# One hand-ordered stream of slots for a two-layer attention and GLU kernel: scores of four heads into one PSUM buffer, values of 16 heads per visit, dense work in units between

## The chip, the cores and the metric

The kernel runs on one core of a Trainium2 chip. The metric is the device time of one execution in microseconds, lower is better. Engines are named as in the profile: PE is TensorE (PEld its weight loads), DVE is VectorE, ACT is ScalarE, POOL is GpSimd, SP is SyncE, which here only issues DMAs.

## The reference: two layers of windowed attention and a gated unit

```python
def _A_ref(x, wqkv, wo):              # S = 2048, D = 512, H = 32 heads of Dh = 16, W = 256
    qkv = (x @ wqkv).reshape(B, S, 3, H, Dh)...
    scores = einsum("bhqd,bhkd->bhqk", q, k) * Dh ** -0.5
    mask = (idx[:, None] - idx[None, :] >= 0) & (idx[:, None] - idx[None, :] < W)
    p = softmax(where(mask, scores, -1e9))
    return einsum("bhqk,bhkd->bhqd", p, v)... @ wo
def _B_ref(x, w_gate, w_up, w_down):  # F = 1792
    return (sigmoid(x @ w_gate) * (x @ w_up)) @ w_down
x = A_x
for _ in range(2):
    x = x + _A_ref(layernorm(x), A_wqkv, A_wo)
    x = x + _B_ref(layernorm(x), B_w_gate, B_w_up, B_w_down)
```

The two layers use the same weights. All tensors are bf16.

## The kernel before

The 2048 tokens are 16 tiles of 128 (index `t`), or four groups of 512 (`tg`). The residual `xsb` stays in SBUF. Work comes in three kinds.

*Dense work* is a list of pieces per emitter. `ProjEmitter` normalises a group (`layernorm_tiles`: statistics, a Newton root of fifteen small DVE steps, then transposes on PE through `ln_tp`), and multiplies it by q, k and v weights into `qT`, `kT` and `Vaug` (values with a column of ones per head, so that the softmax's sums come out of the same matmul). `GluEmitter` does the gate (`gps`, tanh on ACT into `gth`), the up product (`ups`), their product `hT` on DVE, and the down product (`dps`), added to `xsb`. Each unit is 4 matmuls of 512 columns, or 14 for a down tile. Weights of q, k, gate and up are loaded chunk by chunk from DRAM; half of `w_up` is written to a DRAM scratch `wuh` at the start, for sigmoid(g) u = (tanh(g/2) + 1) u/2.

*Attention* goes by key tile `t`: a key tile is met by the queries of tiles t to t+2, 384 columns. `front(t, half)` masks `kTp` out of `kT` (one copy for even and one for odd heads of each 32 rows, so that a head of 16 rows can be one of four row quarters of PE), multiplies four heads into two PSUM tiles `Sps` of two heads each (L353), takes their exp with two ACT instructions (L361) into a ring `PTring` of seven tile slots per head, and multiplies the two diagonal blocks (of queries t and t+2) by a 0/1 mask with one DVE instruction (L365). Then it makes the values of 16 heads for query tile t: head after head in the code (L378), each head a column quarter of PE, up to three key tiles accumulated.

*Normalisation and output*: `norm_half` transposes the values (`tps`), divides by the sums (`Rt`, `On`), transposes back (`tps2`, `OnT`); `oproj_fill` multiplies by `wot` (`OPps`), adds to `xsb`, and then emits dense pieces by a budget of 48 (56 for the last layer's unit).

The order of the instructions on each engine is set by the framework's scheduler, from this program order and the pools' buffers. PSUM: four banks for `Sps`, two for `oq` (values and all of normalisation), two for dense work (`glu`). The first pair of stages runs, then its remaining GLU pieces alone, and the second pair is laid over the last GLU pieces of the first.

Of the kernel before, what the change touches and what calls it, by code (L numbers as in the profile page):

```python
# [11 lines left out]
I32 = mybir.dt.int32  # L12
P = 128
VS = 18
RING_SLOTS = 7
_RING_PS = [(0, 1), (3, 1), (0, 3)]

# [10 lines left out]
class Dims:  # L28
    def __init__(self, S, D, H, Dh, F):
        self.S, self.D, self.H, self.Dh, self.F = S, D, H, Dh, F  # L30
        self.NT = S // P
        self.KT = D // P
        self.FC = F // P
        self.NCQ = D // P
        self.NCK = 2 * self.NCQ
        self.NCO = 2 * self.NCQ
        self.TGW = min(512, S)
        self.NTG = S // self.TGW
        self.NBG = self.TGW // P
        assert S % self.TGW == 0 and self.TGW % P == 0  # L40
        assert Dh == 16 and D == H * Dh and self.NCO == 8 and self.NCQ == 4
        self.VW = H * VS + 32


def make_consts(nc, cpool):
    ident = cpool.tile([P, P], BF16, name="ident")
    nc.gpsimd.memset(ident[:], 0.0)
    nc.gpsimd.affine_select(out=ident[:], in_=ident[:], compare_op=ALU.not_equal, fill=1.0,
                            base=0, pattern=[[-1, P]], channel_multiplier=1)
    maskq = cpool.tile([P, 4, 2, P], BF16, name="maskq")  # L50
    nc.gpsimd.memset(maskq[:], 1.0)
    for u in range(4):
        nc.gpsimd.affine_select(out=maskq[:, u, 0, :], in_=maskq[:, u, 0, :],
                                compare_op=ALU.is_ge, fill=0.0, base=0,
                                pattern=[[1, P]], channel_multiplier=-1)
        nc.gpsimd.affine_select(out=maskq[:, u, 1, :], in_=maskq[:, u, 1, :],
                                compare_op=ALU.is_ge, fill=0.0, base=-1,
                                pattern=[[-1, P]], channel_multiplier=1)
    rm0 = cpool.tile([P, 1], F32, name="rm0")
    nc.vector.memset(rm0[:], 0.0)  # L60
    for m in range(4):
        nc.vector.memset(rm0[32 * m:32 * m + 16, :], 1.0)
    rm1 = cpool.tile([P, 1], F32, name="rm1")
    nc.vector.tensor_scalar(out=rm1[:], in0=rm0[:], scalar1=-1.0, scalar2=1.0,
                            op0=ALU.mult, op1=ALU.add)
    return dict(ident=ident, maskq=maskq, rms=[rm0, rm1])


def rsqrt_eps(nc, pool, var_ap, n, eps=1e-5):
    x = pool.tile([P, n, 1], F32, name="rs_x")  # L70
    nc.vector.tensor_scalar(out=x[:], in0=var_ap, scalar1=eps, scalar2=None, op0=ALU.add)
    t = pool.tile([P, n, 1], I32, name="rs_t")
    nc.vector.tensor_single_scalar(out=t[:], in_=x[:].bitcast(I32), scalar=1, op=ALU.arith_shift_right)
    y = pool.tile([P, n, 1], F32, name="rs_y")
    nc.vector.tensor_scalar(out=y[:].bitcast(I32), in0=t[:], scalar1=0x5F3759DF, scalar2=-1,
                            op0=ALU.subtract, op1=ALU.mult)
    tmp = pool.tile([P, n, 1], F32, name="rs_tmp")
    for _ in range(3):
        nc.vector.tensor_tensor(out=tmp[:], in0=y[:], in1=y[:], op=ALU.mult)
        nc.vector.tensor_tensor(out=tmp[:], in0=tmp[:], in1=x[:], op=ALU.mult)  # L80
        nc.vector.tensor_scalar(out=tmp[:], in0=tmp[:], scalar1=-0.5, scalar2=1.5,
                                op0=ALU.mult, op1=ALU.add)
# [29 lines left out]
class PieceEmitter:  # L112
# [11 lines left out]
    def emit_budget(self, t, budget, pspool):  # L124
        used = 0
# [390 lines left out]
```

## Time and profile before

| | before |
|---|---|
| median of 3 runs | 813.25 us (810.87 to 816.97) |
| the profiled execution, span | 815.3 us, all that the trace gives of its time |
| PE busy | 743.0 us, 91% |
| PEld busy | 327.9 us, 40% |
| DVE busy | 548.8 us, 67% |
| ACT busy | 479.6 us, 59% |
| POOL busy | 24.4 us, 3% |
| mean granted clock of PE | 0.960 |
| first and last exp | 45.4 and 744.1 us |

Busy shares are averages over the stages; what ends a stage is read from its waits and its chain. A matmul's length in the trace holds the way through the array, some 0.16 us beyond its issue, so that neighbours overlap: the price of one is the distance between starts.

### The profile page before, as it was taken

How to read it: one execution, taken by the hardware profiler on the slowest of the kernel's cores; microseconds unless marked ns; L12 is line 12 of the kernel's file. 1: busy time of each engine (PE TensorE's matmuls, PEld its weight loads, DVE VectorE, ACT ScalarE, POOL GpSimd, SP SyncE). 2: the span in 40 equal slices, each digit the busy share in tenths (PEclk: the TensorE clock that was granted, in tenths of full speed). 3: DMA queues.
4: the chain of work that ended last, by engine and by line, in shares of the span. 5: the costliest groups of instructions: out<-in, count | busy, mean ns of one | idle time of the engine just before them, and what ended most of it. 6: DMA issues, size and time to landing. Idle time of an engine off the chain costs nothing.

```text
span 815.3 us, 15745 instructions
## 1 busy us (share of the span) xinstructions
PE 743.0 (91%) x6297; PEld 327.9 (40%) x6400; DVE 548.8 (67%) x1453; ACT 479.6 (59%) x715; POOL 24.4 (3%) x19
## 2 busy tenths in 40 slices
PE   0699999999999999989999999999999999999895
PEld 0334344444444444434334444444444444444442
DVE  5767897657896787676576468473778677766341
ACT  0388776677677765531776755766758676653030
POOL 6000000000000000050000000000000000000000
PEclk9999998999999996999979999899999999899998
DMA  7830111342013300350313223023201330024153
GB/s 257 248 74 9 27 27 27 80 109 47 2 36 70 78 2 2 70 125 14 90 40 70 49 65 110 22 59 78 66 1 27 74 71 13 2 60 109 32 126 104
DMA packets 163050, 52.42 MB, mean 64 GB/s; under 512 B 152224, under 2 KB 161952, under 8 KB 162976
## 3 DMA queue, kind: packets, MB, share of 16 engines
q1 hardware_dynamic: 162976, 51.40, 25.6%
q8 instruction: 50, 0.82, 0.4%
q14 instruction: 24, 0.20, 0.1%
HBM read 47.45 MB, written 3.93 MB: 63 GB/s over the span
## 4 chain that ended last, share of the span: by engine, by line
PE 68%; DVE 13%; ACT 12%; issue 3%; DMA 2%; ACTq 0%; DVEq 0%
PE ups L198 12%; ACT PTring L361 11%; PE gps L192 11%; PE Sps L353 10%; PE OTps L378 9%; PE dps L209 8%; PE proj_ps L258 7%; PE OPps L409 4%; DVE PTring L365 3%; PE proj_ps L269 3%; DVE ln_stats L91 2%; PE tps L390 2%; PE ln_tp L101 1%; DMA wck<-in_A_wqkv_dram 1%; DVE xsb L211 1%
## 5 line engine op out<-in xcount | busy, mean ns | idle before, releaser
L361 ACT ACTIVATE PTring<-Sps 128x768 bf16<-128x768 f32 (+2 forms) x512 | 367.9, 772 | 96.1 <-PE Sps L353 93.0
L365 DVE TENSOR_TENSOR PTring<-PTring,maskq 128x1024 bf16<-128x1024 bf16 x224 | 154.1, 688 | 49.9 <-ACT PTring L361 46.9
L353 PE MATMUL Sps<-qT,kTp 32*128 32x384 bf16 (+2 forms) x1024 | 158.8, 329 | 9.7 <-ACT PTring L361 4.8
L195 ACT ACTIVATE gth<-gps 128x512 bf16<-128x512 f32 x112 | 67.0, 599 | 126.9 <-PE gps L192 107.9
L378 PE MATMUL OTps<-PTring,Vaug 128*32 128x128 bf16 x2880 | 133.1, 228 | 8.2 <-DVE PTring L365 3.6
L200 DVE SCALAR_TENSOR_TENSOR hT<-gth,ups 128x512 bf16<-128x512 bf16 x112 | 76.6, 684 | 81.0 <-PE ups L198 78.6
L198 PE MATMUL ups<-xnB,wgu 128*128 128x512 bf16 x428 | 121.3, 385 | 6.1 <-DVE hT L200 4.4
L192 PE MATMUL gps<-xnB,wgu 128*128 128x512 bf16 x425 | 124.8, 385 | 2.2 <-issue 0.8
L209 PE MATMUL dps<-wd,hT 128*128 128x512 bf16 x425 | 111.5, 384 | 0.9 <-issue 0.3
L378 PEld LDWEIGHTS <-Vaug 128*32 128x32 bf16 x2880 | 74.0, 98 | 90.4 <-issue 87.2
L353 PEld LDWEIGHTS <-kTp 32*128 32x128 bf16 x1024 | 49.4, 91 | 110.5 <-issue 84.6
L258 PE MATMUL proj_ps<-xnTg,wck 128*128 128x512 bf16 x236 | 71.0, 403 | 2.7 <-DMA wck<-in_A_wqkv_dram 1.4
L198 PEld LDWEIGHTS <-wgu 128*128 128x128 bf16 x448 | 40.4, 98 | 56.8 <-issue 21.0
L192 PEld LDWEIGHTS <-wgu 128*128 128x128 bf16 x448 | 41.7, 98 | 46.7 <-issue 8.4
L209 PEld LDWEIGHTS <-hT 128*128 128x128 bf16 x448 | 40.8, 98 | 48.0 <-issue 10.1
L101 PE MATMUL ln_tp<-ident,ln_xn 128*128 128x128 bf16 x256 | 27.6, 238 | 30.0 <-DVE ln_xn L97 26.0
L387 DVE CAST OTs<-OTps 128x512 bf16<-128x512 f32 x64 | 43.8, 685 | 13.7 <-PE OTps L378 13.6
L91 DVE BATCH_NORM_STATS2 ln_stats<-xsb 128x6 f32<-128x512 bf16 x64 | 44.9, 708 | 8.2 <-DMA xsb<-in_A_x_dram 7.8
L339 DVE TENSOR_SCALAR kTp<-kT,rm 128x128 bf16<-128x128 bf16 x256 | 47.1, 246 | 2.6 <-ACT kT L261 2.6
L102 ACT COPY xnTg<-ln_tp 128x512 bf16<-128x512 bf16 x18 | 10.3, 590 | 52.5 <-PE ln_tp L101 52.4
L211 DVE TENSOR_TENSOR xsb<-xsb,dps 128x512 bf16<-128x512 bf16 x32 | 21.8, 682 | 26.8 <-PE dps L209 26.6
L409 PE MATMUL OPps<-wot,OnT 128*128 128x512 bf16 x115 | 35.2, 397 | 1.1 <-issue 0.9
(47 smaller groups left out, 451.4 us busy)
## 6 DMA issues: line engine op xcount, KB each, us to landing
wgu<-in_B_w_gate_dram SPq DMA_DIRECT2D x112, 128.0 KB, 2.4
wgu<-wuh SPq DMA_DIRECT2D x112, 128.0 KB, 2.8
wck<-in_A_wqkv_dram SPq DMA_DIRECT2D x64, 128.0 KB, 2.3
wd<-in_B_w_down_dram SPq DMA_DIRECT2D x2, 1792.0 KB, 8.4
xsb<-in_A_x_dram SPq DMA_DIRECT2D x1, 2048.0 KB, 8.5
out_dram<-xsb SPq DMA_DIRECT2D x1, 2048.0 KB, 7.5
wtmp<-in_B_w_up_dram SPq DMA_DIRECT2D x1, 1792.0 KB, 12.6
wuh<-wtmp SPq DMA_DIRECT2D x1, 1792.0 KB, 7.0
```

What stands on the lines that cost most here:

```text
L91: nc.vector.bn_stats(out=stats[:, ti, :], in_=xsb[:, t0 + ti, :])
L192: nc.tensor.matmul(gps[:], lhsT=wgu[:, kt, 0, :], rhs=xnB[:, kt, :], start=(kt == 0), stop=(kt == d.KT - 1))
L195: nc.scalar.activation(out=th[:], in_=gps[:], func=AF.Tanh, scale=0.5)
L198: nc.tensor.matmul(ups[:], lhsT=wgu[:, kt, 1, :], rhs=xnB[:, kt, :], start=(kt == 0), stop=(kt == d.KT - 1))
L200: nc.vector.scalar_tensor_tensor(out=hT[:, fc, :], in0=th[:], scalar=1.0, in1=ups[:], op0=ALU.add, op1=ALU.mult)
L209: nc.tensor.matmul(dps[:], lhsT=hT[:, fc, tt * P:(tt + 1) * P], rhs=self.wd[:, fc, :], start=(fc == 0), stop=(fc == d.FC - 1))
L258: nc.tensor.matmul(pt[:], lhsT=w[:, kt, :], rhs=xnt[:, kt, :], start=(kt == 0), stop=(kt == d.KT - 1))
L353: nc.tensor.matmul(sps[m % 2][:, m // 2, 0:N], lhsT=kTp[32 * m:32 * m + 32, ck, :], rhs=qT[32 * m:32 * m + 32, cq, t * P:t * P + N], start ...
L361: nc.scalar.activation(out=ring_out, in_=sp_in, func=AF.Exp, scale=scale)
L365: nc.vector.tensor_tensor(out=mout, in0=mout, in1=maskq[:], op=ALU.mult)
L378: nc.tensor.matmul(OT[32 * g:32 * g + 32, col, :], lhsT=Vaug[:, jj, VS * h:VS * h + 32], rhs=ring[:, h, slot, :], start=(jj == jj0), stop= ...
L409: nc.tensor.matmul(ops[:], lhsT=onts[c // 2][:, c % 2, :], rhs=wot[:, c, :], start=(c == 0), stop=(c == d.KT - 1))
```

## The change

The whole body is written anew, as one class `Net` with `tc.manual_schedule()`: every engine runs its instructions in program order. Time is planned in slots. In each of 2 x 128 slots the loop `run` emits, in this order: the scores and the exp of four heads (a tile t has eight such quartets); five slots behind, in every fourth slot, the values of 16 heads; whatever is due from earlier slots (`at`: both halves of normalisation one slot apart, the output product one later, statistics, apply and transposes of the layer norm in three following slots); units of dense work until the planned time of the slot (2050 ns by constants in the code) is full; and last the mask of its scores. The dense units come from a fixed list of streams. Behind slot 255 another 36 slots hold dense units alone.

Moved or replaced besides: `Sps` is one buffer of four banks, and one exp takes 4 x 384 columns; the mask of the query tile t stays on DVE (4 x 128 columns), that of t+2 is a select on POOL; values go key tile by key tile, with the four column quarters next to each other; `kTp` is masked once per group of 512; all of `wqkv`, `wo` and `w_down` stay in SBUF; `wuh` is gone and `w_down` is halved in place; the root is a power on POOL, one token tile at a time; x comes in, and the result goes out, by tiles; all transposes of layer norm and normalisation go through one PSUM bank (`ps_m`), dense units through two (`ps_d`), values through one (`ps_o`).

```diff
+        self.wgup = pool("wgu", 3)
+        self.ps_s = pool("ps_s", 1, True)
+        self.ps_o = pool("ps_o", 1, True)
+        self.ps_d = pool("ps_d", 2, True)
+        self.ps_m = pool("ps_m", 1, True)
...
+    def ln_stats(self, key, t):
...
+        nc.vector.bn_aggr(out=mv[:], in_=st[:])
+        nc.gpsimd.tensor_scalar(out=rs[:, 0:1], in0=mv[:, 1:2], scalar1=1e-5, scalar2=None, op0=ALU.add)
+        nc.gpsimd.tensor_tensor(out=rs[:, 1:2], in0=rs[:, 0:1], in1=self.nhalf[:], op=ALU.pow)
...
+    def ln_later(self, key, t, first=0):
...
+        self.at(first + 1, 0, lambda: self.ln_apply(key, t))
+        self.at(first + 2, KT * T_TR, lambda: self.ln_transpose(key, t))
...
+    def scores(self, L, t, g):
...
+        sps = self.ps_s.tile([P, 4, 512], F32, name="Sps")
+        for m in range(4):
+            nc.tensor.matmul(sps[:, m, 0:N], lhsT=kTp[32 * m:32 * m + 32, cq, e, ko:ko + P],
+                             rhs=self.qT[32 * m:32 * m + 32, cq, t * P:t * P + N],
+                             start=True, stop=True, tile_position=(32 * m, 0))
+        h0 = 8 * cq + e
+        nc.scalar.activation(out=self.ring[:, h0:h0 + 7:2, pj:pj + (nb - 1) * sj + 1:sj, :],
+                             in_=sps[:, :, 0:N].rearrange("p w (b c) -> p w b c", c=P),
+                             func=AF.Exp, scale=1.0 / float(np.sqrt(DH)))
+
+    def mask(self, t, g):
...
+        r0 = self.ring[:, h0:h0 + 7:2, ring_slot(t, 0), :]
+        nc.vector.tensor_tensor(out=r0, in0=r0, in1=self.maskq[:], op=ALU.mult)
+        if t + 2 < NT:
+            r2 = self.ring[:, h0:h0 + 7:2, ring_slot(t, 2), :]
+            nc.gpsimd.affine_select(out=r2, in_=r2, compare_op=ALU.is_ge, fill=0.0, base=-1,
+                                    pattern=[[0, 4], [-1, P]], channel_multiplier=1)
+
+    def values(self, L, t, half, st):
...
+        for col in range(4):
+            co = 4 * half + col
+            for jj in range(jj0, t + 1):
+                Va = self.Vaug[(L * NTG + jj // NBG) % 3]
+                for g in range(4):
+                    h = 4 * co + g
+                    nc.tensor.matmul(OT[32 * g:32 * g + 32, col, :],
...
+        nc.vector.tensor_copy(out=OTs[:], in_=OT[:])
+        self.at(1, 4 * T_TR, lambda: self.norm1(L, t, half, st, OTs))
...
+    def run(self):
...
+            if s < total:
+                L, t, g = s // SLOTS_L, (s % SLOTS_L) // SLOTS_T, s % SLOTS_T
...
+                self.scores(L, t, g)
+                used += T_SC + 2 * T_SW
+                sc = (t, g)
+            v = s - 5
+            if 0 <= v < total and v % 4 == 0:
...
+                self.values(L, t, half, st)
+                used += 48 * 16 + T_SW
+            now = [d for d in self.due if d[0] <= s]
+            self.due = [d for d in self.due if d[0] > s]
+            for _, ns, fn in now:
+                fn()
+                used += ns
+            while True:
+                st_ = next_stream()
+                if st_ is None:
+                    break
+                if used + st_[1][0][0] // 2 > T_SLOT:
+                    break
+                ns, fn = st_[1].pop(0)
+                fn()
+                used += ns
+            if sc is not None:
+                self.mask(*sc)
+            self.slot += 1
```

The order on PE, first before, in the first layer's attention with a GLU group beside it (each matmul follows the load of its weights; `Sps` are scores, `ups` is the up product, `tps` normalisation):

```order
L378 MATMUL OTps<-PTring,Vaug 32x128
L353 LDWEIGHTS kTp
L353 MATMUL Sps<-qT,kTp 128x384
L353 LDWEIGHTS kTp
L353 MATMUL Sps<-qT,kTp 128x384
L198 LDWEIGHTS wgu
L198 MATMUL ups<-xnB,wgu 128x512
L353 LDWEIGHTS kTp
L353 MATMUL Sps<-qT,kTp 128x384
L353 LDWEIGHTS kTp
L353 MATMUL Sps<-qT,kTp 128x384
L400 LDWEIGHTS On
```

And in the new kernel, slot 46, from the end of a quartet of scores (L285) on: layer norm transposes (`ln_tp`), normalisation transposes (`tps`), both into the one bank, and a gate unit:

```order
L285 MATMUL Sps<-qT,kTp_102 128x384
L162 LDWEIGHTS xn
L162 MATMUL ln_tp<-ident,xn 128x128
...
L326 LDWEIGHTS OTs
L326 MATMUL tps<-ident,OTs 128x128
...
L242 LDWEIGHTS wgu
L242 MATMUL gps<-xnT,wgu 128x512
```

Scores stood in pairs between values and single dense matmuls; now they stand four together, and all else comes in whole blocks behind them.

The order on DVE, before, in the same stage (`Rt` and `On` are the division, `OnT` the second transposes' copy):

```order
L365 TENSOR_TENSOR PTring<-PTring,maskq 128x4x2x128
L200 SCALAR_TENSOR_TENSOR hT<-gth,ups 128x512
L387 CAST OTs<-OTps 128x512
L365 TENSOR_TENSOR PTring<-PTring,maskq 128x4x2x128
L393 RECIPROCAL Rt<-tps 128x16
L395 TENSOR_TENSOR On<-tps,Rt 128x256
```

On DVE now, slots 28 to 30, from the output's addition over the statistics to the copy of `ln_tp`:

```order
L352 TENSOR_TENSOR xsb<-xsb,OPps 128x512
L131 BN_STATS ln_stats<-xsb 128x6
L132 BN_AGGR ln_mv<-ln_stats 128x2
L298 TENSOR_TENSOR PTring<-PTring,maskq 128x4x128
L319 CAST OTs<-OTps 128x512
L141 TENSOR_SCALAR xn<-xsb,ln_mv,ln_rs 128x512
L298 TENSOR_TENSOR PTring<-PTring,maskq 128x4x128
L163 COPY xnT<-ln_tp 128x4x128
L329 RECIPROCAL Rt<-tps 128x16
```

POOL before has only constants and the clearing of `Vaug`; now, early in the stream, its selects and the two steps of the root stand in turn:

```order
L133 TENSOR_SCALAR ln_rs<-ln_mv 128x1
L134 TENSOR_TENSOR ln_rs<-ln_rs,nhalf 128x1
L301 AFFINE_SELECT PTring<-PTring 128x4x128
L133 TENSOR_SCALAR ln_rs<-ln_mv 128x1
L134 TENSOR_TENSOR ln_rs<-ln_rs,nhalf 128x1
L301 AFFINE_SELECT PTring<-PTring 128x4x128
```

The mask on DVE has half the columns, the other half went to POOL, and `xn` on DVE now takes its factor from POOL.

701 lines of the change are left out of this document (304 added, 397 removed).

## The prediction

> **What bounds the kernel now.** First the page: span, busy shares, the chain that ended last.
>
> ```profile
> span 815.3 us, 15745 instructions
> ...
> PE 743.0 (91%) x6297; PEld 327.9 (40%) x6400; DVE 548.8 (67%) x1453; ACT 479.6 (59%) x715; POOL 24.4 (3%) x19
> ...
> PE 68%; DVE 13%; ACT 12%; issue 3%; DMA 2%; ACTq 0%; DVEq 0%
> ```
>
> PE is busy for 743 us of 815 and carries two thirds of the chain. The table of waits shows how seldom it is held up:
>
> ```profile
> PE ln_tp L101 <- DVE ln_xn L97: 26.0, 2, 25.1
> ...
> PE Sps L353 <- ACT PTring L361: 4.8, 16, 0.6
> ```
>
> One wait of 25.1 us is the start-up; for scores it waits 4.8 us in the whole run. Stage by stage (columns: stretch, length, PE busy, PEld, DVE, ACT, POOL, granted clock, DMA share, GB/s):
>
> ```profile
> 45.00:354.00 309.00, 296.59 (x2766) 129.86 (x2808) 232.56 (x601) 212.96 (x311) 0.00 (x0) 0.96 0.20 45
> 399.00:744.00 345.00, 330.35 (x2942) 145.02 (x2986) 231.70 (x582) 231.00 (x345) 0.00 (x0) 0.96 0.23 53
> ```
>
> In both attention stages PE is busy 96% of the time, ACT 69 and 67%, DVE 75 and 67%. So **PE's instruction stream is the bound**, and its price is read from single rows. The chain, in order of time, gives 216 ns for a 512-column matmul (7.34 / 34), and the PE timeline shows what lies between kinds (start, length, line, count):
>
> ```profile
> 753.89 7.34 PE dps L209 x34
> ...
> 306.56 1.24 PE L209 MATMUL dps<-wd,hT 128*128 128x512 bf16 x5
> 307.74 0.34 PE L353 MATMUL Sps<-qT,kTp 32*128 32x384 bf16 x4
> 308.01 0.29 PE L378 MATMUL OTps<-PTring,Vaug 128*32 128x128 bf16 x2
> ...
> 303.14 0.52 PE L378 MATMUL OTps<-PTring,Vaug 128*32 128x128 bf16 x19 [0.25 <-DVE ln_mv L93]
> ```
>
> Five `dps` from 306.56 are issued by 307.64, but the scores start at 307.74: **0.10 us for the change of array shape**. Four scores, one in each quarter of the rows, take 0.27 to the next kind: 0.16 for 384 columns once, and 0.10 for the next change. So four at once cost what one costs. Of 19 value matmuls one starts every (0.52 - 0.22) / 18 = 17 ns, 0.22 being the length of the last.
>
> **The change on PE.** The counts of dense matmuls (1856), scores (1024), values (2880) and transposes (640) stay. What goes is splitting: in the instruction order the old stream has 253 score pieces of two and 1238 changes of shape, the new one quartets only and 566. That removes about 670 x 0.10 = 67 us, and, with 446 pieces of scores against 256, 190 passes of 0.16 us, 30 us.
>
> The new stream has 256 slots with scores and 36 behind them. Of the 1856 dense matmuls 48 stand ahead, 300 behind. PE's work in slots 1 to 255: 1508 x 0.216 = 326, 612 transposes x 0.056 (128 columns at the same rate) = 34, 255 x 0.16 = 41, 2832 values x 0.017 = 48, 573 changes x 0.10 = 57: **506 us**, 1.98 a slot.
>
> **The floor of a slot.** `Sps` now has one buffer of four banks, so the scores of a slot wait for the exp of the slot ahead.
>
> ```profile
> 307.81 0.33 PE Sps L353 x4
> 308.13 3.62 ACT PTring L361 x5
> 311.75 0.04 issue
> 311.80 0.32 PE Sps L353
> ...
> L361 ACT ACTIVATE PTring<-Sps 128x768 bf16<-128x768 f32 x448 | 339.1, 813 | 83.0 <-PE Sps L353 80.4 <-PE ln_tp L101 0.2
> ...
> L361 ACT ACTIVATE PTring<-Sps 128x256 bf16<-128x256 f32 x32 | 11.1, 383 | 5.2 <-PE Sps L353 5.0
> ...
> L195 ACT ACTIVATE gth<-gps 128x512 bf16<-128x512 f32 x112 | 67.0, 599 | 126.9 <-PE gps L192 107.9 <-DVE ln_mv L93 8.2 <-issue 6.1
> ...
> 309.52 2.93 ACT L361 ACTIVATE PTring<-Sps 128x768 bf16<-128x768 f32 x4
> ```
>
> The exp costs 813 ns for 768 columns and 383 for 256, 0.84 ns a column: 1.46 us for 1536 (an estimate). With 0.05 from exp to scores, 0.33 of scores and 0.03 back, a slot cannot be under **1.87 us**. Back to back an ACT instruction begins (2.93 - 0.81) / 3 = 0.71 after the last, 0.10 before that one's end; a slot with one tanh or copy (0.60) still fits, one with two takes 1.36 + 2 x 0.50 = 2.36. Slots 23 to 37 have 12 us of PE work and take 28 (+16), slots 1 to 22 gain 8, the 19 later slots with two copies and the thin ones 12. **506 + 36 = 542 us.** ACT as a whole, 430 us by these steps, stays below.
>
> **What the order adds.** `tps`, `tps2` and `ln_tp` share one PSUM bank (`ps_m`), and 39 slots have two or three of them. In such a slot the second user's transposes wait on PE until DVE has read the first, behind the last slot's `hT` and mask:
>
> ```profile
> L200 DVE SCALAR_TENSOR_TENSOR hT<-gth,ups 128x512 bf16<-128x512 bf16 x112 | 76.6, 684 | 81.0 <-PE ups L198 78.6 <-PE gps L192 1.0 <-PE Sps L353 0.7
> ...
> L365 DVE TENSOR_TENSOR PTring<-PTring,maskq 128x1024 bf16<-128x1024 bf16 x224 | 154.1, 688 | 49.9 <-ACT PTring L361 46.9
> ...
> L368 DVE TENSOR_TENSOR PTring<-PTring,maskq 128x512 bf16<-128x512 bf16 x32 | 13.5, 422 | 9.4 <-ACT PTring L361 9.1
> ...
> L339 DVE TENSOR_SCALAR kTp<-kT,rm 128x128 bf16<-128x128 bf16 x256 | 47.1, 246 | 2.6 <-ACT kT L261 2.6
> ...
> L102 DVE COPY xnB<-ln_tp 128x512 bf16<-128x512 bf16 x32 | 12.7, 412 | 1.9 <-PE ln_tp L101 1.8
> ```
>
> From the slot's scores: transposes at 0.26 to 0.48; DVE has 0.68 and 0.42 to finish first, is free near 0.95, copies until 1.36; the second transposes go at 1.40 instead of 0.48, and the dense matmuls behind them as late: 0.9 us, of which a thin slot hides 0.2 under its floor. 39 x 0.75 = **30 us**. A tanh whose gate is the last unit of its slot pushes the next exp by about 0.15 once in 8 slots: 5 us.
>
> **POOL takes half of the masks.** Before, it does nothing inside the stages (0.00 above). Its rows:
>
> ```profile
> L56 POOL TENSOR_SCALAR_AFFINE_SELECT maskq<-maskq 128x128 bf16<-128x128 bf16 x4 | 1.2, 304 | 0.0
> ...
> L287 POOL MEMSET Vaug<- 128x9728 bf16 x2 | 16.4, 8212 | 340.9 <-PE OTps L378 340.9
> ...
> L289 POOL MEMSET Vaug<- 128x512 bf16 x2 | 4.5, 2261 | 0.1
> ```
>
> A select of 512 elements is not in the trace: below, 0.30 (one run of 128); above, 2.26, what 512 scattered elements cost a memset. It has four whole runs, so I take it near the first: 0.95, four times 0.30 less what an instruction pays once; that stays under the slot. The power for `ln_rs` isn't there either: between nothing and the 0.95 of a whole select; I take 0.15, since it writes one element. It sits among the selects, and DVE's `xn` waits for it with mask and `OTs` queued behind, in 64 slots. The two together: between 0 and 64 x 0.95 = 61 us; **12 us**, nearest the short rows. DVE itself gets lighter: from the page's 548.8 go 60 for the masks (154.1 + 13.5 against 256 x 0.422 = 108), 31 for `kTp` (256 steps become 64) and the root's small steps; some 1.6 us a slot are left, under PE's 2.1, so this gains nothing.
>
> **Clock.** Before, the granted clock halves where PE runs only small pieces:
>
> ```profile
> L353 PE MATMUL Sps<-qT,kTp 32*128 32x384 bf16 x10 | 1.7, 326 | 0.6 <-ACT PTring L361 0.4
> L378 PE MATMUL OTps<-PTring,Vaug 128*32 128x128 bf16 x26 | 1.1, 222 | 0.0
> ...
> 309.80:313.20 3.40, 2.79 (x42) 1.42 (x41) 3.23 (x8) 2.98 (x5) 0.00 (x0) 1.00 0.00 0
> 313.20:326.90 13.70, 12.57 (x107) 5.28 (x107) 8.22 (x28) 6.44 (x11) 0.00 (x0) 0.50 0.06 14
> ```
>
> After 3.4 us without one 512-column matmul it stands at 0.50 for 13.7 us. Slots 1 to 5 and 23 to 37 are such stretches: mostly hidden under the exp, but the scores and the first dense slots behind them are slower: **10 us**. All other slots have 4 to 10 dense matmuls in 2 us.
>
> **Both ends.** POOL now has, ahead of the first `ln_rs`, about 2.3 us of constants, three memsets of 8.21 / 4 and three of 2.26 / 4: 10.2 in all, so the first `xn` starts near 11; four rounds of apply, transposes and copy at 1.5 make 17, 12 units of 0.864 and a cold clock 29. First scores at **29** instead of 45. Slot 0: 2. Behind slot 255: 300 x 0.216 + 1 = 66, and 3 for `ups` waiting on `hT` (the chain has 1.02 for some units of 0.86): **69**. End: the last add (0.69), an output of 128 KB instead of 2 MB, and 1.3 us of closing: **4**.
>
> ```profile
> 142.44 1.02 PE ups L198 x4
> ...
> 805.79 0.69 DVE xsb L211
> ...
> wgu<-in_B_w_gate_dram SPq DMA_DIRECT2D x112, 128.0 KB, 2.4
> ...
> out_dram<-xsb SPq DMA_DIRECT2D x1, 2048.0 KB, 7.5
> ```
>
> Loads (2.4 us) are issued two chunks, over 3 us, ahead. **Sum: 29 + 2 + 542 + 30 + 5 + 12 + 10 + 69 + 4 = 703** against the span of 815.3, which lies 2 above the median of the runs, 813.25 (810.87 to 816.97): I predict 701.
>
> **Rivals.** (1) The plan holds, the bank costs nothing since DVE runs ahead: 29 + 2 + 542 + 69 + 4 = 646, with the values at 14 ns 638. DVE's 67 to 75% in the stages of now speaks against it. 0.13.
>
> (2) DVE and POOL get in each other's way. Both are released by the same exp, the mask with two SBUF operands and the select reading SBUF. If one is held for the whole length of the other, DVE's 1.6 us a slot becomes 1.6 + 0.95 = 2.55, above PE's 2.2, and DVE is the bound: 31 + 255 x 2.55 + 73 = 754; in front of a matmul here and there as well, up to 790; half of it in the way, 725. No run yet has both engines active, so nothing in the trace excludes it; that a mask may run while the select waits, and the select while DVE reads PSUM, speaks against it. 0.25 for 720 to 790. The Trainium skill, SBUF — State Buffer, section "Who interferes with whom", states just such a lock: a DVE instruction with two SBUF inputs, or in a 2-port mode, and a GpSimd instruction that reads SBUF exclude each other, and whichever issues second waits in full. By that rule it happens in every slot with a select, and what remains open is only how much of it DVE's idle time absorbs.
>
> (3) Slower than before: the select itself bounds. If the four runs cost like the scattered memset (2.26) and the mask's 0.42 and `ln_rs` come in series, a slot is 2.7 to 2.9; from (821 - 31 - 73) / 255 = 2.8 on the kernel is slower, about 840 at 2.9. The select's row of 0.30 speaks against it. 0.06.
>
> (4) The exp loop does not overlap as planned, and an ACT unit late in each slot delays every exp by 0.5: 2.7 a slot, 790 to 810, no clear change. 0.03.
>
> **How the numbers follow.** My forecast, 670 to 720: 0.53; rivals 0.13, 0.25, 0.06, 0.03. The range reaches from the plan without stalls, 640, to the lock in most slots, 775. A measurement of this kernel tells about 1% (8 us) from no change: faster 0.91, within 0.02, slower 0.07.
>
> **What would show it.** The exp near 1.46 us, slots of 2.1 to 2.2, PE waiting for DVE before `tps` or `ln_tp` for 20 to 40 us in all, first scores near 29, ACT and POOL never late: right. The select over 2 us, DVE busy over 85% in the stages, or masks ending a slot late before the values: wrong, by (2) or (3). If PE waits for `hT` or tanh on the two dense banks (`ps_d`) in most slots, the floor of a slot is mis-sized.

## The result, and the profile after

The changed kernel takes **735.81 us** (median of four runs, 734.18 to 737.87) against 812.06 for the kernel before in the same set (810.69 to 816.97): a ratio of **0.905, 95% interval 0.901 to 0.909**. The prediction was 701 with a range of 640 to 775. The direction and the range held; the time is 35 us above the number, and above the 670 to 720 to which the prediction gave 0.53. What follows is mostly about these 35 us.

The head of the page of the profiled run (737.87 us, span 736.1): busy times, the clock row, and the chain that ended last.

```profile
span 736.1 us, 15556 instructions
PE 628.3 (85%) x6400; PEld 281.4 (38%) x6400; DVE 459.1 (62%) x1015; ACT 456.5 (62%) x465; POOL 219.5 (30%) x367
...
PEclk9959955899999999899999899979999999999999
...
PE 63%; DVE 21%; ACT 8%; POOL 4%; issue 3%; ACTq 0%; POOLq 0%
```

PE is still the engine with the most work, but it is idle for 108 us, and DVE holds 21% of the chain. The clock row shows two dips near its start and some shallow ones later. The answer on the scores tile (minimum, median and maximum in ns, then first and last start in us) gives both ends of the stream:

```profile
L285 PE MATMUL Sps<-qT,kTp x1024: 224/331/498, 30.3 to 660.6; 32*128 32x384 bf16 x149, 32*128 32x256 bf16 x11, 32*128 32x128 bf16 x11
```

First scores at 30.3 (29 in the prediction). From the last scores to the end of the span it is 736.1 - 660.6 = 75.5, where the prediction had 2 of a slot's rest, 69 and 4. So both ends are right, and the miss lies between, in slots 1 to 255: 660.6 - 30.3 - 2 = 628 us instead of 542 + 30 + 5 + 12 + 10 = 599. The groups whose length was an estimate (busy us, mean ns; exp by its shape):

```profile
L289 ACT ACTIVATE PTring<-Sps 128x1536 bf16<-128x1536 f32 x224 | 325.6, 1453 | 105.5 <-PE Sps L285 88.3 <-POOL PTring L301 7.4 <-DVE ln_stats L131 2.9
...
L314 PE MATMUL OTps<-PTring,Vaug 128*32 128x128 bf16 x2880 | 54.6, 227 | 0.0
...
L141 DVE TENSOR_SCALAR xn<-xsb,ln_mv,ln_rs 128x512 bf16<-128x512 bf16 x64 | 38.2, 601 | 12.8 <-POOL ln_rs L134 11.3
L134 POOL TENSOR_TENSOR ln_rs<-ln_rs,nhalf 128x1 f32<-128x1 f32 x64 | 37.1, 580 | 5.3
...
L133 POOL TENSOR_SCALAR ln_rs<-ln_mv 128x1 f32<-128x1 f32 x64 | 18.4, 287 | 218.3 <-DVE ln_mv L132 218.3
```

The exp is 1.453 us (estimate 1.46). The values fill 54.6 us for 2880, 19 ns each (17). The root on POOL is 0.29 + 0.58 = 0.87 us, where the prediction took 0.15 for the power and named no price for the addition ahead of it. And `xn` on DVE has a mean of 0.60 where it had 0.40 before. The waits of PE, in us, times and the longest:

```profile
PE ln_tp L162 <- DVE xn L141: 39.9, 40, 12.0
PE tps L326 <- DVE xnT L163: 26.1, 34, 2.6
PE Sps L285 <- ACT PTring L289: 20.5, 34, 1.8
PE ln_tp L162 <- DVE xnT L163: 5.4, 4, 1.4
PE tps L339 <- DVE xnT L163: 4.8, 6, 1.3
```

Leave out the 12.0 at the start, which lie before the first scores, and 27.9 + 26.1 + 5.4 + 4.8 = 64 us of PE's idle time stand ahead of transposes that wait for DVE; the prediction had said 20 to 40. A slot, from scores to scores, takes 2.47 us on average (median 2.22), where the prediction had said 2.1 to 2.2. How such a slot goes is seen in the timeline (start, length, line, count; the idle time before and its releaser in brackets):

```profile
249.04 0.30 POOL L133 TENSOR_SCALAR ln_rs<-ln_mv 128x1 f32<-128x1 f32 x1 [2.69 <-DVE ln_mv L132]
...
249.42 0.57 POOL L134 TENSOR_TENSOR ln_rs<-ln_rs,nhalf 128x1 f32<-128x1 f32 x1
249.96 1.27 POOL L301 TENSOR_SCALAR_AFFINE_SELECT PTring<-PTring 128x512 bf16<-128x512 bf16 x2
250.03 0.71 DVE L141 TENSOR_SCALAR xn<-xsb,ln_mv,ln_rs 128x512 bf16<-128x512 bf16 x1
...
250.79 0.40 PE L162 MATMUL ln_tp<-ident,xn 128*128 128x128 bf16 x4 [0.28 <-DVE xn L141]
...
251.59 0.41 DVE L163 COPY xnT<-ln_tp 128x512 bf16<-128x512 bf16 x1
252.05 0.38 PE L326 MATMUL tps<-ident,OTs 128*128 128x128 bf16 x4 [0.86 <-DVE xnT L163]
```

Read it downwards. The root ends on POOL at 249.99; `xn` starts at 250.03, beside the selects that stood in line behind the root, and takes 0.71; `ln_tp` waits for it. Then `tps` wants the same PSUM bank, and waits 0.86 us until DVE, after an `hT` and a mask, has copied `ln_tp` out. The dense matmuls of the slot stand behind both. This is the step that the prediction described for the bank, and in front of it a second delay that the prediction had priced far lower.

### The profile page after: what moved, and what is told of

It is laid out like the page before. It is cut to its first block, busy times and chain, and to the rows that moved or that the text cites. A ratio compares the mean times of both kernels' runs of the same rounds, so it can differ in the third digit from the quotient of the medians.

```text
span 736.1 us, 15556 instructions
## 1 busy us (share of the span) xinstructions
PE 628.3 (85%) x6400; PEld 281.4 (38%) x6400; DVE 459.1 (62%) x1015; ACT 456.5 (62%) x465; POOL 219.5 (30%) x367
## 4 chain that ended last, share of the span: by engine, by line
PE 63%; DVE 21%; ACT 8%; POOL 4%; issue 3%; ACTq 0%; POOLq 0%
PE ups L252 12%; PE gps L242 12%; PE dps L264 12%; ACT PTring L289 7%; PE Sps L285 7%; PE proj_ps L186 5%; DVE ln_stats L131 4%; PE OPps L350 4%; PE OTps L314 3%; DVE xn L141 3%; DVE PTring L298 3%; PE tps L326 3%; DVE xnT L163 3%; DVE xsb L352 2%; POOL ln_rs L134 2%
## 5 line engine op out<-in xcount | busy, mean ns | idle before, releaser
L289 ACT ACTIVATE PTring<-Sps 128x1536 bf16<-128x1536 f32 (+2 forms) x256 | 351.4, 1373 | 123.0 <-PE Sps L285 105.8
L301 POOL TENSOR_SCALAR_AFFINE_SELECT PTring<-PTring 128x512 bf16<-128x512 bf16 x224 | 156.6, 708 | 229.9 <-ACT PTring L289 229.9
L298 DVE TENSOR_TENSOR PTring<-PTring,maskq 128x512 bf16<-128x512 bf16 x256 | 123.0, 481 | 36.2 <-ACT PTring L289 35.8
L252 PE MATMUL ups<-xnT,wgu 128*128 128x512 bf16 x448 | 117.5, 385 | 0.5 <-DVE hT L253 0.5
L242 PE MATMUL gps<-xnT,wgu 128*128 128x512 bf16 x448 | 117.0, 384 | 0.0
L285 PE MATMUL Sps<-qT,kTp 32*128 32x384 bf16 (+2 forms) x1024 | 89.6, 338 | 20.7 <-ACT PTring L289 20.5
L285 PEld LDWEIGHTS <-kTp 32*128 32x128 bf16 x1024 | 30.5, 91 | 129.2 <-issue 128.9
L186 PE MATMUL proj_ps<-xnT,wq 128*128 128x512 bf16 x256 | 67.5, 402 | 3.4 <-ACT kt L193 1.9
L162 PE MATMUL ln_tp<-ident,xn 128*128 128x128 bf16 x256 | 28.7, 242 | 45.7 <-DVE xn L141 39.9
L314 PE MATMUL OTps<-PTring,Vaug 128*32 128x128 bf16 x2880 | 54.6, 227 | 0.0
L326 PE MATMUL tps<-ident,OTs 128*128 128x128 bf16 x256 | 26.7, 231 | 26.4 <-DVE xnT L163 26.1
L314 PEld LDWEIGHTS <-Vaug 128*32 128x32 bf16 x2880 | 43.0, 100 | 11.5 <-issue 10.4
L141 DVE TENSOR_SCALAR xn<-xsb,ln_mv,ln_rs 128x512 bf16<-128x512 bf16 x64 | 38.2, 601 | 12.8 <-POOL ln_rs L134 11.3
```

Source lines behind the costliest of these rows:

```text
L186: nc.tensor.matmul(pt[:], lhsT=self.wq[:, kt, c0:c0 + P], rhs=xnT[:, kt, :], start=(kt == 0), stop=(kt == KT - 1))
L242: nc.tensor.matmul(ps[:], lhsT=w[:, kt, 0, :], rhs=xnT[:, kt, :], start=(kt == 0), stop=(kt == KT - 1))
L252: nc.tensor.matmul(ps[:], lhsT=w[:, kt, 1, :], rhs=xnT[:, kt, :], start=(kt == 0), stop=(kt == KT - 1))
L285: nc.tensor.matmul(sps[:, m, 0:N], lhsT=kTp[32 * m:32 * m + 32, cq, e, ko:ko + P], rhs=self.qT[32 * m:32 * m + 32, cq, t * P:t * P + N], s ...
L289: nc.scalar.activation(out=self.ring[:, h0:h0 + 7:2, pj:pj + (nb - 1) * sj + 1:sj, :], in_=sps[:, :, 0:N].rearrange("p w (b c) -> p w b c" ...
L298: nc.vector.tensor_tensor(out=r0, in0=r0, in1=self.maskq[:], op=ALU.mult)
```

## The experiments

Two theories stood at the start. **A**: the shared bank `ps_m`, and an `xn` that comes late, are the loss. **B**: DVE and POOL hold each other up (`xn` and some masks are longer than they were). **C** was a third candidate, the half clock. Three sets of kernels were run; the kernel before had medians of 812.38, 811.0 and 816.59 in them, so that differences across sets are given by ratios too. Names with `bank` or `late` build on an earlier experiment.

**e1, transposes to slots of their own.** The normalisation's transposes go to the next slot, at least two ahead, in which no transpose of the attention output stands, and the apply to the slot ahead of that; its small tiles get eight buffers instead of four.

```
-        self.at(first + 1, 0, lambda: self.ln_apply(key, t))
-        self.at(first + 2, KT * T_TR, lambda: self.ln_transpose(key, t))
+        s = self.slot + first + 2
+        while s % 4 in (2, 3) or s in self.tr_slots:
+            s += 1
+        self.tr_slots.add(s)
+        self.at(s - 1 - self.slot, 0, lambda: self.ln_apply(key, t))
+        self.at(s - self.slot, KT * T_TR, lambda: self.ln_transpose(key, t))
```

> The layer norm's transposes go to the next slot, at least two after the statistics, in which no normalisation transposes stand (slots 0 or 1 modulo 4), and the apply step to the slot before it; nothing else changes. Theory A (the shared bank and the late xn cost it): slots of the kind 46 take 3.41 us on average over slots 38 to 255 against a floor of 1.87; they fall to 1.9 to 2.2, PE's waits for xn and xnT (55 us in the attention slots) fall under 15, and the time is 685 to 705 us. Theory B (DVE is held up by POOL in every slot): the waits turn up elsewhere, 725 to 737 us. Theory C (the half clock at the start holds the loss): 728 to 737 us.

Measured: 720.43 us (719.67 to 721.19), ratio 0.887 (0.883 to 0.891), between the theories. The waits of `tps` are gone, but new ones stand in the list of PE:

```profile
PE Sps L290 <- ACT PTring L294: 31.4, 33, 1.8
PE ln_tp L167 <- DVE xn L142: 20.5, 9, 11.9
PE gps L247 <- DVE xnT L168: 9.4, 8, 1.8
PE proj_ps L191 <- ACT kt L198: 9.2, 15, 0.9
PE v_ps L208 <- ACT Vaug L211: 8.1, 10, 0.9
```

The order of units has shifted, and now many slots hold two projection units whose copies both go to ACT. Its timeline shows one:

```profile
270.47 1.46 ACT L294 ACTIVATE PTring<-Sps 128x1536 bf16<-128x1536 f32 x1
...
271.81 0.59 ACT L211 CAST Vaug<-v_ps 128x512 bf16<-128x512 f32 x1
...
272.45 1.02 PE L208 MATMUL v_ps<-wq,xnT 128*128 128x512 bf16 x4 [0.81 <-ACT Vaug L211]
...
273.41 0.34 PE L290 MATMUL Sps<-qT,kTp 32*128 32x384 bf16 x4
273.51 0.58 ACT L211 CAST Vaug<-v_ps 128x512 bf16<-128x512 f32 x1 [1.11 <-PE v_ps L208]
...
274.00 1.46 ACT L294 ACTIVATE PTring<-Sps 128x1536 bf16<-128x1536 f32 x1
```

The copy waits behind the exp, the second unit for the copy, the next scores for the unit, and the second copy delays the next exp: 274.00 - 270.47 = 3.5 us for a slot that the prediction costed at 2.36. The changed kernel has five such slots, 3.4 to 3.5 us long. A move that removes one wait by shifting the whole order is a poor test of that wait; e2 is the clean one.

**e2, another bank alone.** The order stays; only the bank of `ln_tp` differs.

```
-        self.at(first + 2, KT * T_TR, lambda: self.ln_transpose(key, t))
+        self.at(first + 2, KT * T_TR, lambda: self.ln_transpose(key, t, self.ps_d))
```

> Only the PSUM bank changes: the layer norm's transposes go through the two dense banks instead of the one that normalisation uses. Theory A in its narrow form (the sharing of the bank alone): PE's 31 us of waits of tps for xnT vanish, the 25 us of ln_tp for xn stay: 705 to 715 us. If xn's lateness is what counts and the bank only hides it, 725 to 737 us.

Measured: **698.02 us** (696.13 to 699.5), ratio 0.859 (0.856 to 0.863): 37.8 us less than the changed kernel, and below the range of theory A. The first rows of PE's waits:

```profile
PE ln_tp L162 <- DVE xn L141: 39.5, 41, 11.9
PE Sps L285 <- ACT PTring L289: 21.9, 37, 1.8
```

`tps <- xnT` is gone, and `ln_tp <- xn` has not moved. The two waits add up, they do not hide each other. A holds, at 38 us.

Not all of it is waiting. By the two pages PE's idle time falls by 24.6 us (107.8 to 83.2), and its busy time by 14.2 (628.3 to 614.1) for the same matmuls; the mean granted clock rises from 0.942 to 0.966. The changed kernel shows how this comes about, in slot 182 (PE's rows, then a stretch with the columns of the prediction's stage table):

```profile
490.24 0.59 PE L162 MATMUL ln_tp<-ident,xn 128*128 128x128 bf16 x4 [1.34 <-DVE xnT L163]
491.34 0.59 PE L326 MATMUL tps<-ident,OTs 128*128 128x128 bf16 x4 [0.51 <-DVE xnT L163]
491.72 2.34 PE L264 MATMUL dps<-wd,hT 128*128 128x512 bf16 x5
```

```profile
490.00:496.80 6.80, 6.05 (x25) 2.50 (x25) 2.15 (x7) 1.45 (x1) 0.34 (x1) 0.50 0.00 0
```

From the scores at 487.06 to 491.72 PE has waits and small matmuls alone; from 490.0 on the granted clock is 0.50 for 6.8 us, and five `dps` take 2.34 us, where five took 1.24 in the kernel before. Between 300 us and the last scores the changed kernel has 23.8 us at half clock, each stretch in or right behind a slot with such waits, and e2 has 6.8.

**e3, no select on POOL.** The whole mask, 128 x 1024, is one DVE multiplication again; POOL keeps the root.

```
-        nc.vector.tensor_tensor(out=r0, in0=r0, in1=self.maskq[:], op=ALU.mult)
-            nc.gpsimd.affine_select(out=r2, in_=r2, compare_op=ALU.is_ge, fill=0.0, base=-1, ...)
+            r = self.ring[:, h0:h0 + 7:2, pj:pj + 2 * sj + 1:2 * sj, :]
+            nc.vector.tensor_tensor(out=r, in0=r, in1=self.maskb[:], op=ALU.mult)
```

> The select leaves POOL: DVE masks both blocks at once, 128x1024, as before the change; POOL keeps the root alone. Theory B (DVE and POOL shut each other out, and that is the loss): xn falls from a median of 0.71 us to 0.40, no mask is stretched, and the time falls by 10 us or more, to 726 or less. Theory A: the lock costs DVE some 30 us in all, which the longer masks (0.69 for 0.42, 224 times: 60 us) more than eat: 735 to 755 us.

Measured: 742.89 us (740.07 to 747.55), ratio 0.915 (0.910 to 0.920), as A said. Its DVE groups and PE's first wait:

```profile
L309 DVE TENSOR_TENSOR PTring<-PTring,maskb 128x1024 bf16<-128x1024 bf16 x224 | 152.6, 681 | 32.3 <-ACT PTring L298 32.3
...
L150 DVE TENSOR_SCALAR xn<-xsb,ln_mv,ln_rs 128x512 bf16<-128x512 bf16 x64 | 25.9, 409 | 18.1 <-POOL ln_rs L143 17.1
```

```profile
PE ln_tp L171 <- DVE xn L150: 45.5, 39, 15.0
```

Without a select beside it `xn` takes 0.409 again instead of 0.601, so the mutual delay exists. But DVE pays 0.26 us more for each mask, and PE waits for `xn` 45.5 us instead of 39.9 (3.0 of this at the start, where POOL has one more mask to build, so that the first scores come 2.1 us later). Those 2.1 aside, the kernel is some 5 us slower: the select on POOL is worth its price. The run doesn't show what the delay costs, since it takes away one load of DVE and adds another.

**e4, no thin slots for the clock.** Three matmuls of 512 columns, whose result nobody reads, in slots 1 to 5 and 23 to 37.

```
+            if sc is not None and (0 < s < 6 or 22 < s < 38):
+                dm = self.ps_d.tile([P, D], F32, name="idle_ps", tag="d")
+                for c in range(3):
+                    nc.tensor.matmul(dm[:], lhsT=self.wq[:, c, 0:P], rhs=self.wot[:, c, :], start=(c == 0), stop=(c == 2))
```

> Three more 512-column matmuls, whose result nobody reads, in each of slots 1 to 5 and 23 to 37, that is 60 matmuls or 13 us of PE added, in slots that wait for the exp anyway. Theory C (the half clock): the granted clock stays at 1.0 there (now 0.82 and 0.57 in the two stretches to 127 us), slots 6, 7, 14, 22, 38 and 39 lose 1 to 3 us each, and the time falls by 10 to 20 us, to 716 to 726. If the half clock is hidden under the exp: 733 to 742.

Measured: 730.35 us (729.65 to 731.84), ratio 0.899 (0.896 to 0.903), 5.5 us less than the changed kernel and between the two cases. The two kernels in the same stretches (window; length; PE, PEld, DVE, ACT, POOL busy; granted clock), the changed kernel first:

```profile
29.00:89.00 60.00, 45.11 (x403) 19.52 (x401) 40.56 (x98) 43.86 (x48) 25.25 (x43) 0.83 0.00 1
89.00:129.00 40.00, 24.61 (x317) 12.74 (x318) 24.48 (x58) 24.75 (x19) 16.23 (x28) 0.56 0.01 1
```

```profile
29.00:89.00 60.00, 46.81 (x415) 19.72 (x412) 40.51 (x98) 43.22 (x46) 24.88 (x43) 0.89 0.00 1
89.00:129.00 40.00, 29.97 (x365) 13.89 (x364) 23.97 (x58) 24.54 (x19) 16.89 (x28) 0.87 0.01 1
```

The clock of the thin stretch goes from 0.56 to 0.87, and slots 23 to 37 take 32.7 us instead of 33.3: the time hardly moves. In the second window of the changed kernel the exp holds 33% of the chain and PE waits 8.4 us for it, so a faster PE gains little there. The ten slots behind, 38 to 47, gain 2.9 us, slots 6 to 22 lose 2.6, and the slots from 48 on, where nothing was added, gain 6.0: they have 10.2 us at half clock instead of 23.8. So e4 does not price the thin slots by itself; e11 does that better.

**e5, values quarter by quarter.** Within a visit the loop over the column quarters goes outside the loop over key tiles.

```
-            for jj in range(jj0, t + 1):
-                for g in range(4):
+            for g in range(4):
+                for jj in range(jj0, t + 1):
```

> The changed kernel with one difference: within a visit the value matmuls go through one quarter of the columns after the other (group, then key block), as before the change, instead of changing quarter at every matmul. Theory A (the order of quarters carries the gain of the values part): 2880 value matmuls were busy 133.1 us before and 54.6 us after, 78 us apart; 62 of the 64 visits lie in slots with scores, and a visit's 1.2 us more passes the floor of its slot almost wholly: 60 to 75 us more, 795 to 812. Theory B (what made them short is that a visit has 48 in a row with one change of shape, in any order): 733 to 742.

Measured: 738.48 us (735.4 to 739.75), ratio 0.910 (0.905 to 0.915): no difference from the changed kernel (0.901 to 0.909). Its value matmuls fill 55.4 us against 54.6. The order of the quarters carries nothing; what is left is the other half of that edit, 48 in a row. That the 133.1 us which this group shows before come from its short pieces is not tested by itself.

**e6, two exps.** `Sps` in two buffers of two banks, two exps of 768 columns a slot; the four scores still go in a row.

```
-        sps = self.ps_s.tile([P, 4, 512], F32, name="Sps")
+        sps = [self.ps_s.tile([P, 2, 512], F32, name="Sps") for _ in range(2)]
```

> The changed kernel with the four scores of a slot in two buffers of two banks and two exps of 768 columns instead of one of 1536; the scores still go four in a row, one in each quarter of the rows. Theory A (one exp of 1536 is part of the gain): two exps back to back take 0.71 + 0.81 = 1.52 us where one takes 1.45, 224 slots x 0.07 = 16 us more of ACT, and the dense work that waits behind the second pair of scores waits as long: 745 to 752. Theory B (PE is the bound in most slots, and two buffers let the first pair go early): no change or a gain of up to 10 us, 725 to 738.

Measured: 736.57 us (732.92 to 737.9), ratio 0.908 (0.903 to 0.914): no difference. PE's wait for the exp falls, and the other waits stay (41.0 us for `xn`, 26.5 for `tps`):

```profile
PE Sps L285 <- ACT PTring L291: 6.2, 21, 1.1
```

**e7, apply and transposes one slot later.** On top of e2, in `ln_later`:

```
-        self.at(first + 1, 0, lambda: self.ln_apply(key, t))
-        self.at(first + 2, KT * T_TR, lambda: self.ln_transpose(key, t, self.ps_d))
+        self.at(first + 2, 0, lambda: self.ln_apply(key, t))
+        self.at(first + 3, KT * T_TR, lambda: self.ln_transpose(key, t, self.ps_d))
```

> The changed kernel with the normalisation's transposes in the dense banks instead of the one shared with the transposes of the attention output (as the version that took 698.0), and besides the applying of the normalisation, and its transposes, one slot later than that, so that the root on POOL (0.29 + 0.57 us) has a slot more. With the bank alone PE still waits 39.5 us for xn before these transposes, 11.9 of it once at the start. Theory A (the root on POOL is late and PE pays for it; the prediction priced this at 12 us): the other 27 us go, the time is 671 to 680. Theory B (PE loses there only what the floor of the slot hides anyway, and DVE has as much to do in the next slot): 690 to 700.

Measured: **668.25 us** (668.12 to 669.82), ratio 0.824 (0.820 to 0.828): 29.8 us less than e2, or 28.6 by the ratios, and below the range of theory A. The tile `xn` in e2, then in e7 (minimum, median, maximum in ns), with PE's waits for it:

```profile
L141 DVE TENSOR_SCALAR xn<-xsb,ln_mv,ln_rs x64: 381/705/853, 11.5 to 634.3; 128x512 bf16<-128x512 bf16 x64
...
  PE ln_tp L162: 39.5, 41
```

```profile
L141 DVE TENSOR_SCALAR xn<-xsb,ln_mv,ln_rs x64: 398/409/726, 11.5 to 623.3; 128x512 bf16<-128x512 bf16 x64
...
  PE ln_tp L162: 19.8, 12
```

Several things go at once. PE's wait falls from 27.6 to 7.9 us behind the start. `xn` is short more often: 28 of the 64 take more than 0.55 us, where 42 did. And the order shifts: four of the five long slots with two copies on ACT are gone, with 4.8 us of PE's waits for such copies; 85 more dense matmuls stand between the first and the last scores (1585 instead of 1500), and the stretch behind the last scores takes 58.0 us instead of 76.3. So e7, like e1, is no clean test of one wait. By the two pages PE's idle time falls by 24.6 us (83.2 to 58.6): 19.7 in this wait, and most of the rest in those for copies. Its busy time falls by 6.1 (614.1 to 608.0); the two stretches at half clock that e2 has between 300 us and its last scores, 3.4 us each, are gone. What of the 19.7 is the root, and what the longer `xn`, e7 doesn't show; e10 bounds the root's part.

**e8, e2 with the filled slots of e4.**

> The changed kernel with the normalisation's transposes in the dense banks, and besides three matmuls of 512 columns, whose result nobody reads, in each of slots 1 to 5 and 23 to 37, where PE has little dense work. With the bank alone the clock stands at half for 13.7 us from 36.2, 10.2 from 90.8 and 17 from 104.5, some 41 us. Theory A (the clock costs the first dense slots behind these stretches): 5 to 8 us less than 698, as the same matmuls took 5.5 from the changed kernel: 690 to 694. Theory B (the slots from 104 on are bound by exp, half clock or not, and the added matmuls cost what they save): 696 to 701.

Measured: 694.57 us (692.95 to 696.83), ratio 0.856 (0.852 to 0.861): 3.5 us less than e2 (2 by the ratios, whose intervals overlap), and between the theories.

**e9, the price of a change of array shape.** On top of e7, one matmul of 32 rows and 8 columns ahead of each gate and up unit, into the bank that the unit overwrites.

```
+        nc.tensor.matmul(ps[:, 0:8], lhsT=self.wq[0:32, 0, 0:P], rhs=self.wq[0:32, 0, 0:8],
+                         start=True, stop=True, tile_position=(0, 0))
```

> The version that took 668.25 (normalisation's transposes in the dense banks and one slot later), and besides, ahead of each gate and up unit, one matmul of 32 rows and 8 columns into the unit's own bank, which the unit then overwrites. Such a matmul stands between dense ones, so it adds changes of array shape and almost no columns: 330 more of them between the first and the last scores (890 against 560). Theory A (a change of shape costs PE 0.10 us, as the prediction read from two gaps, and removing 670 of them was two thirds of what the change saves on PE): 33 us more, less what the floor of thin slots hides: 692 to 702. Theory B (the gaps that the prediction read as changes were something else, for instance the time until the first result): at most 5 us more, 667 to 673.

Measured: 703.51 us (700.52 to 704.01), ratio 0.863 (0.857 to 0.869): 35 us more than e7, or 31 by the ratios, and 1.5 above the range of theory A. The 224 small matmuls make 386 changes, 330 of them between the first and the last scores and 56 behind, so that a change costs **0.08 to 0.09 us** over the whole run, thin slots included. PE's timeline in the glu part shows it row by row:

```profile
303.41 1.04 PE L244 MATMUL gps<-xnT,wgu 128*128 128x512 bf16 x4
304.38 0.17 PE L253 MATMUL ups<-wq 32*128 32x8 bf16 x1
304.49 1.04 PE L256 MATMUL ups<-xnT,wgu 128*128 128x512 bf16 x4
```

Four dense matmuls are 4 x 0.216 = 0.86 us; the small one starts 0.97 behind their first, and the next dense one 0.11 behind it. So 0.11 us into the other shape, and about as much out of it, with eight columns of work. The run tests changes between the whole array and 32 rows alone. For the column quarters of the values there is no such run; a row of the changed kernel agrees: 48 values from 248.34, 0.85 us long, so that the last starts at 248.97, and the next dense matmul at 249.13. That is 0.16 us for 128 columns, which alone take 0.06.

**e10, a shorter root.** On top of e2, the root is one instruction on POOL.

```
-        nc.gpsimd.tensor_scalar(out=rs[:, 0:1], in0=mv[:, 1:2], scalar1=1e-5, scalar2=None, op0=ALU.add)
-        nc.gpsimd.tensor_tensor(out=rs[:, 1:2], in0=rs[:, 0:1], in1=self.nhalf[:], op=ALU.pow)
+        nc.gpsimd.tensor_tensor(out=rs[:, 1:2], in0=mv[:, 1:2], in1=self.nhalf[:], op=ALU.pow)
```

> The version with the normalisation's transposes in the dense banks alone (698.0), with the root made in one instruction on POOL (the power, 0.57 us) instead of two (0.29 + 0.57): the addition of 1e-5 to the variance is left out, which changes nothing visible in the result. Theory A (the root's latency on POOL is on the path in the 40 slots in which PE waits for xn): 40 x 0.29 = 12 us less, 684 to 690. Theory B (moving the apply by a slot saved 30 us by spreading DVE's work, not through POOL): 695 to 700.

Measured: 688.68 us (687.92 to 689.81), ratio 0.844 (0.840 to 0.849): 9 us less than e2, 12 by the ratios, about 1.6 of it ahead of the first scores (28.8 instead of 30.4). PE's waits:

```profile
PE ln_tp L161 <- DVE xn L140: 20.5, 27, 1.5
PE ln_tp L161 <- POOL ln_rs L133: 11.5, 1, 11.5
```

The second row is the wait at the start under another name. The first has fallen from 27.6 to 20.5. So an instruction of 0.29 us on one element, on an engine that is busy for a third of the span, is worth 9 to 12 us: theory A.

**e11, e7 with the filled slots.** The best version but for a tie.

> The version that took 668.25, with the three unread matmuls in slots 1 to 5 and 23 to 37 as well. Its clock stands at half for 13.7 us from 35.3 and for 27.3 us from 89.9. Theory A (worth 3.5 to 5.5 us as in the two versions before): 662 to 665. Theory B (these slots are bound by exp): 667 to 670.

Measured: **663.92 us** (663.08 to 665.17), ratio 0.814 (0.809 to 0.819), 4.3 us less than e7 (8 by the ratios). Of some 41 us at half clock ahead of 125 us, 3.4 are left, and slots 23 to 37 with the ten behind them take 52.7 us instead of 56.1.

**e12, e11 with two exps.**

> The same with the scores of a slot in two buffers of two banks and two exps of 768 columns. Split alone, in the changed kernel, they made no difference, but PE's wait for the exp fell from 20.5 to 6.2 us there, while two other waits stood on the path; these are gone now. Theory A (the floor of a slot, scores that wait for the whole exp of the slot ahead, is the next bound): 12 to 16 us less than with one exp, 646 to 652. Theory B (ACT's 0.07 us more in 224 slots, 16 us, eats it): 660 to 668.

Measured: 662.54 us (662.14 to 664.11), ratio 0.813 (0.808 to 0.817): the time of theory B, no difference from e11. PE's wait for the exp is 4.7 us (14.5 in e11), and the time is the same: a wait that becomes shorter is no gain by itself.

## Why the prediction was right, and where its sum failed

| Term | Predicted, us | Measured, us | By |
|---|---|---|---|
| First scores | 29 | 30.3 | changed kernel |
| From the last scores to the end | 2 + 69 + 4 | 75.5 | changed kernel |
| Change of array shape, each | 0.10 | 0.11 in the rows, 0.08 to 0.09 over the run | e9 |
| Exp of 1536 columns | 1.46 | 1.453 | changed kernel |
| Shared bank `ps_m` | 30 | 38 | e2 |
| Root on POOL, `xn` late | 12 | 20 of PE's waits; 29 to 30 with the shifted order | e7 (9 to 12 for the addition alone: e10) |
| Half clock in the thin slots | 10 | 2 to 8 | e4, e8, e11 |
| Late tanh | 5 | not measured apart | |

**The direction** came out of the right place. PE's instruction stream was the bound before, and what the change takes out of it is what the prediction counted. Of the 79 us that the span loses, 68 lie between the first and the last scores (698.3 to 630.3), 15 ahead of them and -3 behind. The price of 0.10 us, read off two gaps in a timeline, is the term on which 67 us rested, and e9 measures it in another way, a little lower over the whole run. The 30 us for scores four at a time have no run of their own. The values at 17 ns nearly held (19 each, 54.6 us for 2880), for the row of 48 and not for the neighbouring quarters. Of the other signs that the prediction named, the exp and the first scores came as said; the slots and PE's waits were longer, and POOL was late: behind the start DVE waited for the root 15 times, 5.7 us in all.

**The step that failed is "POOL takes half of the masks".** It bounded the power "between nothing and the 0.95 of a whole select" and took 0.15 "since it writes one element". The power was inside the bounds, but took 0.58; the addition ahead of it, which had no price of its own, took 0.29. That is as long as the select of 128 elements before (0.30), so for an addition on one element this row was near; nothing in the trace of before shows a power. And `xn`, whose length the sum left as it was (0.40 before), took 0.71 at the median. Both lie one behind the other ahead of `ln_tp`, so the term was 12, where PE's waits that e7 takes away are 20 and the whole step, with the order that it shifts, 29 to 30. The upper bound of 61 had contained it.

**The bank** was described as it happens (the timeline at 250.79 to 252.05 is the predicted sequence), and was mis-sized by 8 us: 30 against 38. The prediction priced the wait and not the clock that falls behind it: it expected the half clock in slots 1 to 5 and 23 to 37 alone, and PE's busy time, with the same matmuls, is 14.2 us less in e2. A late `xn` also makes the transposes of `ln_tp` and their copy late; no run separates that.

**Rival (2)**, DVE and POOL in each other's way, gave 720 to 790, and the time fell into that. Its mechanism is there: a DVE instruction that starts inside a select is held. It does not do all that the rival priced: 44 of the 64 `xn` and 45 masks start inside a select, and not one in every slot (97 of the 224 selects overlap a mask at all), the median of the masks is 0.418 (0.42 before), and their mean 0.481. In all DVE is busy some 12 us longer with `xn` and 16 with the masks, DVE is busy for 62% of the span and not the bound, and the largest single loss is the bank. So the time is that of the rival, and the cause for the greater part is not. The Trainium skill, SBUF — State Buffer, section "Who interferes with whom", says that a DVE instruction in a 2-port mode and a GpSimd instruction exclude each other, whoever issues second waiting for the whole of the other. The trace agrees, closely, for `xn` and for the mask with its two SBUF operands:

```profile
37.31 0.64 POOL L301 TENSOR_SCALAR_AFFINE_SELECT PTring<-PTring 128x512 bf16<-128x512 bf16 x1
37.62 0.47 DVE L141 TENSOR_SCALAR xn<-xsb,ln_mv,ln_rs 128x512 bf16<-128x512 bf16 x1
...
440.20 0.64 POOL L301 TENSOR_SCALAR_AFFINE_SELECT PTring<-PTring 128x512 bf16<-128x512 bf16 x1 [1.07 <-ACT PTring L289]
440.41 0.70 DVE L298 TENSOR_TENSOR PTring<-PTring,maskq 128x512 bf16<-128x512 bf16 x1
```

This `xn` ends 0.14 us behind the end of the select, and this mask 0.27. So do the others: the 39 `xn` with more than 0.3 us of it left end 0.143 to 0.146 us behind it, and 44 of the 45 masks 0.273 to 0.277. An `xn` that starts 0.08 us into a select of 0.64 thus takes 0.56 + 0.145 = 0.71, the median above. What the holding costs in time, no run shows by itself.

**Rival (1)**, the plan without stalls at 646, is what e11 and e12 approach: 663.92 and 662.54. The three steps (e2, e7, e11) took off 72 us together, against the 52 predicted for these terms: 20 of the 35 us. **The other 15 stay open**: they are what e11 stands above 649, the sum without these terms. The two-copy slots are no explanation, since e11 has lost four of five; nor is the wait of scores for the exp, by e12.

**Rival (3)** fell with the select's median of 0.637 us, near the row of 0.30 and far from 2.26, and **rival (4)** with the exp loop: two slots in three have a period of 2.05 to 2.45 us.

## What to carry to other kernels

When a list of engines is put in order by hand, look for resources that two steps of one slot share: a PSUM bank that two small transposes use in turn made PE wait 0.9 us for a copy, 38 us in all, and giving one of them another bank cost nothing. Look also at what a wait does to the clock: here 14 of those 38 us are PE's busy time, the same matmuls at a lower mean clock. Price a helper step on an idle engine by its latency on the path and not by its busy time: POOL was idle for 70% of the span, and yet 9 to 12 us went with one of its two one-element instructions. Where a timeline shows a constant gap between kinds of matmuls, count the changes of kind in the instruction order: at 0.10 us each they cost more than a matmul of 128 columns (0.06).

## What the runs showed of the hardware

- A change between the whole array and 32 rows costs PE 0.11 us in each direction in the rows, with eight columns of work between, and 0.08 to 0.09 over the whole run (e9).
- An instruction on one element costs POOL 0.29 us (addition) or 0.58 us (power); a select of 128 x 512 in bf16 0.637.
- `xn`, 128 x 512 in bf16, takes 0.41 us on DVE alone. Started inside a select on POOL with more than 0.3 us of it left, it ends 0.145 us behind the end of the select, and a mask with two SBUF operands, started inside one, ends 0.275 us behind it (changed kernel).
- After 4.7 us with waits and small matmuls alone, PE's granted clock stood at 0.50 for 6.8 us, and five matmuls of 512 columns took 2.34 us instead of 1.24 (changed kernel, slot 182).
- Four column quarters interleaved or one after the other: 54.6 and 55.4 us for 2880 value matmuls (e5).
- Slots 23 to 37 take 33.3 us at a granted clock of about 0.50, and 32.7 us at 0.89 with three more dense matmuls each (e4).
